# One value load per unit in a buffer of its own, in a cached-attention decode step

## The chip, the cores and the metric

The kernel runs on one core of a Trainium2 chip. The metric is the device time in microseconds of one execution; the time of a kernel is the median of several. A profile is taken from one further execution, and its span (first to last instruction) is a little shorter than that execution's time.

The core has five engines that run side by side and wait for one another by semaphores: TensorE (PE, matmuls; PEld is its weight load), VectorE (DVE), ScalarE (ACT), GpSimd (POOL) and SyncE (SP). Sixteen DMA engines move data between HBM and the on-chip memory, which has 128 partitions.

## The reference

One decode step, one query token for each of two batch entries, mixes cached attention with a gated MLP:

```python
x = A_x                                   # (2, 1, 512)
xn = _layernorm(x, axis=-1)
s = _A_ref(xn, A_k_cache, A_v_cache, A_wq, A_wo)
g = _silu(_B_ref(xn, B_w1, B_w2, B_w3, B_w4))
return x + s * g
```

In `_A_ref`, `q = x @ wq` has 32 heads of 128, and the caches have 8 heads of 32768 tokens by 128, so four query heads share a cache head. Scores are scaled by 128 ** -0.5, a softmax runs over the 32768 tokens, the result is multiplied with V and then with `wo` (4096 x 512). K and V are bfloat16, 2 x 8 x 32768 x 128 each, 134 MB apiece. With one token, the shifted branch of `_B_ref` contributes nothing, so the MLP is what remains: layernorm, `w3` (512 x 1792), gelu, `w4` (1792 x 512), a residual, then silu.

## The kernel before

**Units and pieces.** A unit is one batch entry and one cache head: 16 units, each with 8 MB of K and 8 MB of V. K and V of a unit come in two pieces of 16384 tokens (`NCH` is 2), 4 MB each. In a piece partition p holds 128 tokens that follow one another, 32 KB per partition, so a piece is one contiguous 4 MB of HBM.

**Loads and buffers.** The list `loads` (built ahead of `issue`) gives the order of all large transfers: K of unit 0 with `wq` between its pieces, `w3`, `w4`, and then for each unit n by turns a piece of K of unit n + 1 and a piece of V of unit n, at last `wo`. All are issued on SP's queue and share one pool of five buffers of 32 KB per partition (`SLOTS`). `issue(i)` takes the next buffer in turn, so a load waits until the load five places earlier has been used up. The main loop works through `loads` in the same order and calls `issue(i + SLOTS)` after each. The last V piece goes as two transfers of 2 MB, and `wo` as four (2, 1, 0.5 and 0.5 MB).

**Work on a K piece (`k_job`).** DVE transposes it in four blocks (`transposed`, L286, into `ktb`, two buffers). PE multiplies each block with the query weights `qz`, eight matmuls of 128x512 to a block (`scores`, L234), one block behind DVE (`LAG`). Scores of a unit collect in PSUM. After the last block `softmax_front` takes the row maxima (L248) and appends two steps to a list, `glue`: `step1` transposes the maxima on PE (L253) and reduces them, `step2` broadcasts the maximum (L264), runs the exponentials on ACT (L271) and transposes the probabilities on DVE (L275). `k_job` pops one step of `glue` after each block.

**Work on a V piece (`v_job`).** PE multiplies the piece with the probabilities, 32 matmuls (L313), four column strips of the array at a time. After the first four of them it flushes the K blocks that are still waiting for their scores. After the second piece `unit_end` copies the accumulator (`acs`, L335) and appends the unit's finish (`ot`, L339 to L346) to `glue`.

**Order.** The order of instructions on each engine is the order in which the code issues them (`manual_schedule`). An instruction that waits holds up everything behind it on its engine, and the same goes for a DMA issue on SP.

**Start and end.** The query (`q_job`) is made once the first two K blocks are transposed; the MLP (`mlp_job`, L407 to L439) runs when `w4` is in, between K of unit 0 and K of unit 1. At the end `o_final` reorders the heads, `wo_job` (L365) multiplies with `wo`, and the gated sum goes out.

The functions that the change touches, with what calls them:

Of the kernel before, what the change touches and what calls it, by code (L numbers as in the profile page):

```python
# [9 lines left out]
BF16 = mybir.dt.bfloat16  # L10
# [4 lines left out]

UT = 128
GT = 16
SLOTS = 5
KTB = 2
KG = 2  # L20
LAG = 1
# [3 lines left out]
def kernel(  # L25
# [14 lines left out]
    nc = tc.nc  # L40

    B, Sq, D = A_x.shape
    _, Hkv, Sk, Dh = A_k_cache.shape
    HD = A_wq.shape[1]
    Hq = HD // Dh
    rep = Hq // Hkv
    Fdim = B_w3.shape[1]
    assert Sq == 1 and B == 2 and Dh == 128 and rep == 4 and D == 512 and Fdim % 128 == 0
    DK = D // 128
    FK = Fdim // 128  # L50
    CH = UT * 128
    NCH = Sk // CH
    NB = UT // GT
    NS = 32 // rep
# [8 lines left out]
    NU = len(units)  # L63

    ctx.enter_context(tc.manual_schedule())
    head = ctx.enter_context(tc.tile_pool(name="head", bufs=1))
    slots = ctx.enter_context(tc.tile_pool(name="slots", bufs=SLOTS))
    pers = ctx.enter_context(tc.tile_pool(name="pers", bufs=1))
    kt_pool = ctx.enter_context(tc.tile_pool(name="ktb", bufs=KTB))
    p_pool = ctx.enter_context(tc.tile_pool(name="prob", bufs=2))  # L70
# [10 lines left out]
    w3_v = B_w3.rearrange("(p k) f -> p k f", k=DK)  # L81
    w4_v = B_w4.rearrange("(p f) d -> p f d", f=FK)
    NR = HD // 128
    wo_v = A_wo.rearrange("(p r) d -> p (r d)", r=NR)

    loads = [("K", 0, 0), ("wq",)]
    loads += [("K", 0, c) for c in range(1, NCH)]
    loads += [("w3",), ("w4",)]
    for n in range(NU):
        for c in range(NCH):  # L90
            if n + 1 < NU:
                loads.append(("K", n + 1, c))
            loads.append(("V", n, c))
    wo_cuts = [0, NR // 2, 3 * NR // 4, NR - 4, NR]
    loads += [("wo",)]
    tiles = {}

    def issue(i):
        if i >= len(loads):
            return  # L100
        what = loads[i]
        t = slots.tile([128, UT * Dh], BF16, tag="slot", name=f"slot_{what[0]}")
        if what[0] in ("K", "V"):
            b, g = units[what[1]]
            c = what[2]
            src = A_k_cache if what[0] == "K" else A_v_cache
            sv = src[b, g, c * CH:(c + 1) * CH, :].rearrange("(p t) d -> p (t d)", p=128)
            w = UT * Dh // 2 if what == ("V", NU - 1, NCH - 1) else UT * Dh
            for w0 in range(0, UT * Dh, w):
                nc.sync.dma_start(out=t[:, w0:w0 + w], in_=sv[:, w0:w0 + w])  # L110
        elif what[0] == "wq":
            nc.sync.dma_start(
                out=t[:, 0:DK * HD].rearrange("p (k f) -> p k f", k=DK), in_=wq_v)
        elif what[0] == "wo":
            for r0, r1 in zip(wo_cuts, wo_cuts[1:]):
                nc.sync.dma_start(out=t[:, r0 * D:r1 * D], in_=wo_v[:, r0 * D:r1 * D])
        elif what[0] == "w3":
            nc.sync.dma_start(
                out=t[:, 0:DK * Fdim].rearrange("p (k f) -> p k f", k=DK), in_=w3_v)
        else:  # L120
            nc.sync.dma_start(
                out=t[:, 0:FK * D].rearrange("p (f d) -> p f d", f=FK), in_=w4_v)
        tiles[what] = t

    issue(0)
    x_bf = tmp.tile([B, D], BF16, tag="row", name="x_bf")
    nc.scalar.dma_start(out=x_bf[:, :], in_=A_x[:, 0, :])
    x4 = pers.tile([128, 128], BF16)
    nc.gpsimd.memset(x4[:, :], 0.0)
    for b in range(B):  # L130
        nc.scalar.dma_start(out=x4[b:128:32, :], in_=A_x[b, 0, :].rearrange("(j c) -> j c", j=4))
    for i in range(1, SLOTS):
        issue(i)


    ident = head.tile([128, 128], BF16)
# [10 lines left out]
    for k in range(4):  # L147
        wb, par = k // 2, k % 2
        src = ident[:, :].rearrange("p (wb w two) -> p wb two w", wb=2, two=2)[:, wb, par, :]
# [7 lines left out]
        out=headm[:, :], in_=identf[:, :].rearrange("p (x h) -> p h x", h=rep), axis=AX.X, op=ALU.max)  # L157
# [39 lines left out]
    for j, src in enumerate((xn_bf, ln2_bf)):  # L197
        sv = src[:, :].rearrange("b (p k) -> b k p", k=DK)
        for k in range(DK):
            nc.tensor.transpose(  # L200
                out=treg[:, (j * DK + k) * B:(j * DK + k + 1) * B],
                in_=sv[:, k, :], identity=ident[0:B, 0:B])
# [11 lines left out]
    unit_st = {}  # L214
    waiting = []
    glue = []
# [73 lines left out]
    def flush(keep):  # L290
        while len(waiting) > keep:
            scores(*waiting.pop(0))
# [10 lines left out]
            if glue:  # L303
                glue.pop(0)()

    def v_job(n, c):
        vv = tiles[("V", n, c)][:, :].rearrange("p (e i t d) -> p e t i d", i=4, t=GT, d=Dh)
        for e in range(NB // 4):
            half, r0 = (c * NB + e * 4) // NS, (c * NB + e * 4) % NS * rep
            pT = unit_st[n]["pT"]  # L310
            for t in range(GT):
                j = t % 4
                nc.tensor.matmul(  # L313
                    acc[32 * j:32 * j + 16, :].rearrange("p (i d) -> p i d", d=Dh),
                    lhsT=pT[:, half * GT + t, r0:r0 + 16],
                    rhs=vv[:, e, t, :, :],
                    start=(c == 0 and e == 0 and t < 4),
                    stop=(c == NCH - 1 and e == NB // 4 - 1 and t >= GT - 4),
                    tile_position=(0, 32 * j),
                )  # L320
                if e == 0 and t == 3:
                    flush(0)
                elif t % 4 == 3 and glue and n == NU - 1:
                    glue.pop(0)()
        if c == NCH - 1:
            unit_end(n)

    s_ps = s_psp.tile([128, 128], F32)
# [31 lines left out]
    def wo_job():  # L360
        w = tiles[("wo",)]
        for r in range(NR):
            for j in range(4):
                c0 = r * D + 128 * j
                nc.tensor.matmul(  # L365
                    s_ps[32 * j:32 * j + B, :], lhsT=oP[:, :, r], rhs=w[:, c0:c0 + 128],
                    start=(r == 0), stop=(r == NR - 1), tile_position=(0, 32 * j))
# [31 lines left out]
                out=qz[32 * i:32 * i + 32, n % 2, :, c0:c0 + rep], in_=qp[32 * i:32 * i + 32, :, b, g, :])  # L399

    def mlp_job():
        w3 = tiles[("w3",)][:, 0:DK * Fdim].rearrange("p (k q f) -> p k f q", k=DK, f=FK)
        w4 = tiles[("w4",)][:, 0:FK * D].rearrange("p (f d) -> p f d", f=FK)
        hT_ps = mi_psp.tile([128, FK * B], F32, tag="mi", name="hT")
        for f in range(FK):
            for k in range(DK):
                nc.tensor.matmul(  # L407
                    hT_ps[:, f * B:(f + 1) * B],
                    lhsT=w3[:, k, f, :],
                    rhs=xT[:, DK + k, :],  # L410
                    start=(k == 0), stop=(k == DK - 1),
                )
        hf = pers.tile([128, FK * B], F32)
        nc.vector.tensor_copy(out=hf[:, :], in_=hT_ps[:, :])
        x2 = pers.tile([128, FK * B], F32)
        nc.vector.tensor_mul(out=x2[:, :], in0=hf[:, :], in1=hf[:, :])
        nc.vector.tensor_scalar(out=x2[:, :], in0=x2[:, :], scalar1=0.044715, scalar2=1.0, op0=ALU.mult, op1=ALU.add)
        inner = pers.tile([128, FK * B], F32)
        nc.vector.tensor_mul(out=inner[:, :], in0=hf[:, :], in1=x2[:, :])
        th = pers.tile([128, FK * B], F32)  # L420
        nc.scalar.activation(out=th[:, :], in_=inner[:, :], func=ACT.Tanh, scale=GELU_C)
        nc.vector.tensor_scalar(out=th[:, :], in0=th[:, :], scalar1=0.5, scalar2=0.5, op0=ALU.mult, op1=ALU.add)
        h_bf = pers.tile([128, FK * B], BF16)
        nc.vector.tensor_mul(out=h_bf[:, :], in0=hf[:, :], in1=th[:, :])  # L424
        h2_ps = mi_psp.tile([B, D], F32, tag="mi", name="h2")
        for f in range(FK):
            nc.tensor.matmul(  # L427
                h2_ps[0:B, :],
                lhsT=h_bf[:, f * B:(f + 1) * B],
                rhs=w4[:, f, :],  # L430
                start=(f == 0), stop=(f == FK - 1),
            )
        t_f = tmp.tile([B, D], F32, tag="row", name="t_f")
        nc.vector.tensor_add(out=t_f[:, :], in0=xn[:, :], in1=h2_ps[0:B, :])
        sig = tmp.tile([B, D], F32, tag="row", name="sig")
        nc.scalar.activation(out=sig[:, :], in_=t_f[:, :], func=ACT.Sigmoid)
        nc.vector.tensor_mul(out=g_sb[:, :], in0=t_f[:, :], in1=sig[:, :])
        for b in range(B):
            nc.scalar.dma_start(  # L439
                out=g4[b:128:32, :], in_=g_sb[b:b + 1, :].rearrange("b (j c) -> b j c", j=4))  # L440


    for i, what in enumerate(loads):
        if what[0] == "K":
            k_job(what[1], what[2])
        elif what[0] == "V":
            if what[2] == 0:
                while glue and unit_st[what[1]]["pT"] is None:
                    glue.pop(0)()
            v_job(what[1], what[2])  # L450
        elif what == ("w4",):
            mlp_job()
        elif what[0] == "wo":
            while glue:
                glue.pop(0)()
            o_final()
            wo_job()
        issue(i + SLOTS)

    sg = tmp.tile([128, 128], F32, tag="row", name="sg")  # L460
    nc.vector.tensor_tensor(out=sg[:, :], in0=s_ps[:, :], in1=g4[:, :], op=ALU.mult)
# [34 lines left out]
```

## Time and profile before

| what | value |
|---|---|
| median of three runs | 661.0 us (660.96 to 661.13) |
| the profiled execution | 660.7 us |
| its span | 658.9 us |
| granted TensorE clock, mean | 0.82 |
| data read from HBM | 280.50 MB |
| 4 MB loads of K / V | 32 / 31, and two of 2 MB of V |
| median from issue to landing, K / V | 39.9 us / 34.3 us |

A page of the profile gives each engine's busy time and share of the span, then the span in 40 equal slices with one digit of busy share for each, then DMA queues with packets, megabytes and the share of the 16 engines' time that their packets took. The stage table gives, for each stretch of the span, the busy time of PE, PEld, DVE, ACT and POOL, the granted clock, the DMA share and GB/s. In the timeline a line begins with start and length in us; SPq is SP's queue issuing a DMA; what stands in brackets is how long the engine had been idle and what ended that.

### The profile page before, as it was taken

What the parts mean: (1) busy time and instruction counts of PE and PEld (TensorE: products, weight loads), DVE (VectorE), ACT (ScalarE), POOL (GpSimd) and SP (SyncE); (2) the same over time, 40 slices, a digit from 0 to 9 for tenths busy, and PEclk for the clock granted to TensorE, in tenths of its full rate; (3) what the DMA queues carried; (4) which work ended last, traced back from release to release, by engine and by line L of the source; (5) the groups of instructions that cost most, each with busy time, mean ns of one, the idle gap of its engine ahead of it and who ended that gap; (6) DMA issues with size and microseconds to landing.
All of it is one profiled execution on the core that took longest, in us unless ns stands there. A gap on an engine that the chain in (4) does not pass through costs nothing.

```text
span 658.9 us, 5935 instructions
## 1 busy us (share of the span) xinstructions
PE 420.9 (64%) x2595; PEld 173.8 (26%) x2595; DVE 365.4 (55%) x312; ACT 38.5 (6%) x104; POOL 2.2 (0%) x10
## 2 busy tenths in 40 slices
PE   0587767477575657746567784657668565764775
PEld 0342223132221223222122332223222222322233
DVE  6174856556654645655555654555565455465531
ACT  1103010000000000000000000000000100000000
POOL 1000000000000000000000000000000000000000
PEclk9997877987786898777898686888868688887776
DMA  9999999999999999999999999999999999999995
GB/s 382 420 438 441 417 444 433 426 443 420 442 431 430 439 426 437 432 427 442 427 436 429 430 443 424 437 432 430 443 422 437 432 431 438 425 436 437 430 425 246
DMA packets 10445, 280.88 MB, mean 426 GB/s; under 512 B 1194, under 2 KB 1204, under 8 KB 1460
## 3 DMA queue, kind: packets, MB, share of 16 engines
q1 hardware_dynamic: 10376, 280.50, 98.8%
q8 instruction: 20, 0.33, 0.2%
q14 instruction: 5, 0.04, 0.0%
q10 hardware_dynamic: 44, 0.01, 0.0%
HBM read 280.50 MB, written 0.00 MB: 426 GB/s over the span
## 4 chain that ended last, share of the span: by engine, by line
DMA 71%; PE 17%; DVE 9%; issue 1%; ACT 1%; SPq 0%; DVEq 0%; ACTq 0%
DMA slot_K<-in_A_k_cache_dram 62%; PE sc L234 12%; DVE ktb L286 7%; DMA slot_wo<-in_A_wo_dram 6%; DMA slot_wq<-in_A_wq_dram 3%; PE acc L313 3%; DVE pT L275 1%; ACT pr L271 1%; PE h L427 1%; PE qT L374 1%; PE hT L407 1%; PE bc L264 0%; DVE nb L268 0%; ACT qz L398 0%; DVE Sm L278 0%
## 5 line engine op out<-in xcount | busy, mean ns | idle before, releaser
L234 PE MATMUL sc<-ktb,qz 128*128 128x512 bf16 x1024 | 310.9, 460 | 198.4 <-DVE ktb L286 196.7
L286 DVE STREAM_TRANSPOSE ktb<-slot_K 128x2048 uint32<-128x2048 uint32 x128 | 292.1, 2298 | 169.9 <-DMA slot_K<-in_A_k_cache_dram 142.3
L234 PEld LDWEIGHTS <-qz 128*128 128x128 bf16 x1024 | 110.7, 112 | 369.0 <-issue 305.6
L313 PE MATMUL acc<-slot_V,pT 128*16 128x512 bf16 x1024 | 70.8, 399 | 5.4 <-DMA slot_V<-in_A_v_cache_dram 5.4
L313 PEld LDWEIGHTS <-pT 128*16 128x16 bf16 x1024 | 23.2, 90 | 54.9 <-issue 34.6
L248 DVE TENSOR_REDUCE m<-sc 128x1 f32<-128x1024 f32 x16 | 19.5, 1221 | 29.8 <-PE sc L234 29.8
L398 ACT COPY qz<-qp 32x16 bf16<-32x16 bf16 x64 | 12.9, 201 | 330.0 <-PE sc L234 308.3
L275 DVE STREAM_TRANSPOSE pT<-pr 128x1024 bf16<-128x1024 bf16 x16 | 19.9, 1245 | 21.2 <-ACT pr L271 21.2
L271 ACT ACTIVATE pr<-sc,nb 128x1024 bf16<-128x1024 f32 x16 | 17.8, 1113 | 234.1 <-DVE nb L268 234.1
L335 DVE COPY acs<-acc 128x512 f32<-128x512 f32 x16 | 11.1, 692 | 14.1 <-PE acc L313 14.1
L341 PE MATMUL ot<-sel,acs 128*128 128x4 f32 x128 | 18.2, 265 | 0.3 <-DVE acs L335 0.3
L341 PEld LDWEIGHTS ot<-sel,acs 128*128 128x128 f32 x128 | 17.2, 209 | 0.4 <-DVE acs L335 0.4
L268 DVE TENSOR_SCALAR nb<-bc 128x1 f32<-128x1 f32 x16 | 2.5, 158 | 22.4 <-PE bc L264 22.4
L374 PE MATMUL qT<-xT,slot_wq 128*128 128x2 bf16 x128 | 3.6, 165 | 12.1 <-DMA slot_wq<-in_A_wq_dram 12.1
L264 PEld LDWEIGHTS bc<-ones_f,gx 1*128 1x128 f32 x32 | 6.5, 250 | 12.9 <-issue 10.9
L264 PE MATMUL bc<-ones_f,gx 1*128 1x1 f32 x32 | 7.8, 311 | 1.0 <-DVE gx L258 1.0
L339 PEld LDWEIGHTS ot<-Sm,ones_f 128*128 128x128 f32 x32 | 6.2, 203 | 3.8 <-issue 1.7
L253 PE MATMUL mT<-identf,m 128*1 128x128 f32 x16 | 4.4, 276 | 3.6 <-DVE m L248 3.6
L374 PEld LDWEIGHTS <-slot_wq 128*128 128x128 bf16 x128 | 3.5, 104 | 12.2 <-DMA slot_wq<-in_A_wq_dram 12.2
L427 PE MATMUL h<-slot_w,h_bf 128*2 128x512 bf16 x14 | 4.9, 525 | 1.6 <-DVE h_bf L424 1.6
L345 DVE RECIPROCAL rc<-ot 128x4 f32<-128x4 f32 x16 | 2.4, 149 | 5.5 <-PE ot L341 5.5
L200 PE MATMUL treg<-ident,xn_bf 2*128 2x2 bf16 x4 | 0.3, 174 | 7.8 <-DVE xn_bf L188 7.8
(70 smaller groups left out, 62.4 us busy)
## 6 DMA issues: line engine op xcount, KB each, us to landing
slot_K<-in_A_k_cache_dram SPq DMA_DIRECT2D x32, 4096.0 KB, 39.9
slot_V<-in_A_v_cache_dram SPq DMA_DIRECT2D x31, 4096.0 KB, 34.3
slot_wq<-in_A_wq_dram SPq DMA_DIRECT2D x1, 4096.0 KB, 21.4
slot_V<-in_A_v_cache_dram SPq DMA_DIRECT2D x2, 2048.0 KB, 29.5
slot_w<-in_B_w_dram SPq DMA_DIRECT2D x2, 1792.0 KB, 39.0
slot_wo<-in_A_wo_dram SPq DMA_DIRECT2D x1, 2048.0 KB
slot_wo<-in_A_wo_dram SPq DMA_DIRECT2D x1, 1024.0 KB
slot_wo<-in_A_wo_dram SPq DMA_DIRECT2D x2, 512.0 KB, 38.7
```

What stands on the lines that cost most here:

```text
L234: nc.tensor.matmul(sc[:, half, :].rearrange("p (t k) -> p t k", k=32), lhsT=qz[:, n % 2, k, off:off + 128], rhs=kv[:, k // 2, k % 2, :, :] ...
L248: nc.vector.tensor_reduce(out=m1[:, :], in_=st["sc"][:, :, :].rearrange("p x k -> p (x k)"), axis=AX.X, op=ALU.max)
L264: nc.tensor.matmul(bc[:, :], lhsT=st["gx"][:, :, :].rearrange("o x h -> o (x h)"), rhs=ones_f[0:1, 0:1], start=True, stop=True)
L271: nc.scalar.activation(out=pr[:, :], in_=st["sc"][:, :, :].rearrange("p x k -> p (x k)"), func=ACT.Exp, bias=nb[:, 0:1], scale=inv_sqrt_dh ...
L275: nc.vector.transpose(out=pT[:, :, :].rearrange("p t r -> p (t r)"), in_=pr[:, :])
L286: nc.vector.transpose(out=ktb[:, :], in_=kw)
L313: nc.tensor.matmul(acc[32 * j:32 * j + 16, :].rearrange("p (i d) -> p i d", d=Dh), lhsT=pT[:, half * GT + t, r0:r0 + 16], rhs=vv[:, e, t, ...
L335: nc.vector.tensor_copy(out=acs[:, :], in_=acc[:, :])
L341: nc.tensor.matmul(ot[:, 0:rep], lhsT=acs[:, i * Dh:(i + 1) * Dh], rhs=sel[:, i, :], start=(i == 0), stop=(i == 3))
L374: nc.tensor.matmul(qT_ps[:, h * B:(h + 1) * B], lhsT=w[:, k * HD + h * Dh:k * HD + (h + 1) * Dh], rhs=xT[:, k, :], start=(k == 0), stop=(k ...
L398: nc.scalar.copy(out=qz[32 * i:32 * i + 32, n % 2, :, c0:c0 + rep], in_=qp[32 * i:32 * i + 32, :, b, g, :])
L427: nc.tensor.matmul(h2_ps[0:B, :], lhsT=h_bf[:, f * B:(f + 1) * B], rhs=w4[:, f, :], start=(f == 0), stop=(f == FK - 1),)
```

## The change

V of a unit comes in one load of 8 MB, 64 KB per partition, into a buffer of its own (`vslot`, one buffer of 64 KB per partition). K keeps three buffers of 32 KB (`KSLOTS`). The sum, 160 KB per partition, is that of the five buffers before.

- In a unit partition p now holds 256 tokens that follow one another. A V row is 64 KB of contiguous HBM; a K piece takes 32 KB out of each 64 KB.
- The order of loads becomes: both pieces of K of unit n + 1, then V of unit n.
- `wq`, `w3` and `w4` share the V buffer at different columns ahead of the first V.
- The last unit's V (now called `Z`) comes into K's buffers: one piece of 4 MB, then the second piece as two transfers of 2 MB into one buffer, and `wo` into the third.
- A load is issued when the buffer that it takes has been used up, in the order of the list (`ready`, `issue_ready`). A V load thus waits for the work on the V before it, and the loads behind it in the list wait too.
- Ahead of a unit's V matmuls, the waiting K blocks get their scores and all of `glue` is popped. Then the 64 matmuls follow in one run.

```diff
-SLOTS = 5
+KSLOTS = 3
...
-    slots = ctx.enter_context(tc.tile_pool(name="slots", bufs=SLOTS))
+    slots = ctx.enter_context(tc.tile_pool(name="slots", bufs=KSLOTS))
+    vslot = ctx.enter_context(tc.tile_pool(name="vslot", bufs=1))
...
+    W3, W4 = DK * HD, DK * HD + DK * Fdim
...
     for n in range(NU):
-        for c in range(NCH):
-            if n + 1 < NU:
-                loads.append(("K", n + 1, c))
-            loads.append(("V", n, c))
+        if n + 1 < NU:
+            loads += [("K", n + 1, c) for c in range(NCH)]
+        if n + 1 < NU:
+            loads.append(("V", n))
+        else:
+            loads += [("Z", n, c) for c in range(NCH)]
...
-    def issue(i):
-        if i >= len(loads):
-            return
-        what = loads[i]
-        t = slots.tile([128, UT * Dh], BF16, tag="slot", name=f"slot_{what[0]}")
-        if what[0] in ("K", "V"):
+    kload = [w for w in loads if w[0] in ("K", "Z", "wo")]
+    done = set()
+
+    def ready(what):
+        if what[0] in ("K", "Z", "wo"):
+            j = kload.index(what)
+            return j < KSLOTS or kload[j - KSLOTS] in done
+        if what[0] == "V":
+            return ("V", what[1] - 1) in done if what[1] else ("w4",) in done
+        return True
+
+    def issue_ready():
+        while loads and ready(loads[0]):
+            issue(loads.pop(0))
+
+    def issue(what):
+        if what[0] in ("K", "Z", "wo"):
+            t = slots.tile([128, UT * Dh], BF16, tag="slot", name=f"slot_{what[0]}")
+        elif what[0] in ("wq", "V"):
+            t = vslot.tile([128, NCH * UT * Dh], BF16, tag="v", name=f"slot_{what[0]}")
+        else:
+            t = tiles[("wq",)]
+        if what[0] in ("K", "V", "Z"):
             b, g = units[what[1]]
-            c = what[2]
             src = A_k_cache if what[0] == "K" else A_v_cache
-            sv = src[b, g, c * CH:(c + 1) * CH, :].rearrange("(p t) d -> p (t d)", p=128)
-            w = UT * Dh // 2 if what == ("V", NU - 1, NCH - 1) else UT * Dh
-            for w0 in range(0, UT * Dh, w):
-                nc.sync.dma_start(out=t[:, w0:w0 + w], in_=sv[:, w0:w0 + w])
+            sv = src[b, g, :, :].rearrange("(p t) d -> p (t d)", p=128)
+            if what[0] == "V":
+                nc.sync.dma_start(out=t[:, :], in_=sv)
+            else:
+                c0, w = what[2] * UT * Dh, UT * Dh
+                if what == ("Z", NU - 1, NCH - 1):
+                    w = w // 2
+                for w0 in range(0, UT * Dh, w):
+                    nc.sync.dma_start(out=t[:, w0:w0 + w], in_=sv[:, c0 + w0:c0 + w0 + w])
...
-    def v_job(n, c):
-        vv = tiles[("V", n, c)][:, :].rearrange("p (e i t d) -> p e t i d", i=4, t=GT, d=Dh)
-        for e in range(NB // 4):
-            half, r0 = (c * NB + e * 4) // NS, (c * NB + e * 4) % NS * rep
+    def v_job(n, t, c0, c1):
+        nx = NB // 4
+        vv = t[:, :].rearrange("p (x i t d) -> p x t i d", i=4, t=GT, d=Dh)
+        for x in range(c0 * nx, c1 * nx):
+            half, r0 = x * 4 // NS, x * 4 % NS * rep
...
-                if e == 0 and t == 3:
-                    flush(0)
-                elif t % 4 == 3 and glue and n == NU - 1:
-                    glue.pop(0)()
-        if c == NCH - 1:
+        if c1 == NCH:
             unit_end(n)
...
-    for i, what in enumerate(loads):
+    for what in order:
         if what[0] == "K":
             k_job(what[1], what[2])
         elif what[0] == "V":
-            if what[2] == 0:
-                while glue and unit_st[what[1]]["pT"] is None:
-                    glue.pop(0)()
-            v_job(what[1], what[2])
+            flush(0)
+            while glue:
+                glue.pop(0)()
+            v_job(what[1], tiles[what], 0, NCH)
+        elif what[0] == "Z":
+            while glue:
+                glue.pop(0)()
+            v_job(what[1], tiles[what], what[2], what[2] + 1)
...
-        issue(i + SLOTS)
+        done.add(what)
+        issue_ready()
```

More of the change, by code (lines that the diff above doesn't have):

```diff
@@ L118, in issue @@
             nc.sync.dma_start(
-                out=t[:, 0:DK * Fdim].rearrange("p (k f) -> p k f", k=DK), in_=w3_v)
+                out=t[:, W3:W3 + DK * Fdim].rearrange("p (k f) -> p k f", k=DK), in_=w3_v)
         else:
             nc.sync.dma_start(
-                out=t[:, 0:FK * D].rearrange("p (f d) -> p f d", f=FK), in_=w4_v)
+                out=t[:, W4:W4 + FK * D].rearrange("p (f d) -> p f d", f=FK), in_=w4_v)
         tiles[what] = t
-    issue(0)
+    order = list(loads)
+    issue(loads.pop(0))
     x_bf = tmp.tile([B, D], BF16, tag="row", name="x_bf")
@@ L131 @@
         nc.scalar.dma_start(out=x4[b:128:32, :], in_=A_x[b, 0, :].rearrange("(j c) -> j c", j=4))
-    for i in range(1, SLOTS):
-        issue(i)
+    issue_ready()
     ident = head.tile([128, 128], BF16)
@@ L304, in k_job @@
                 glue.pop(0)()
-    def v_job(n, c):
-        vv = tiles[("V", n, c)][:, :].rearrange("p (e i t d) -> p e t i d", i=4, t=GT, d=Dh)
-        for e in range(NB // 4):
-            half, r0 = (c * NB + e * 4) // NS, (c * NB + e * 4) % NS * rep
+    def v_job(n, t, c0, c1):
[3 more added lines that the diff above has]
+            half, r0 = x * 4 // NS, x * 4 % NS * rep
             pT = unit_st[n]["pT"]
-            for t in range(GT):
-                j = t % 4
+            for u in range(GT):
+                j = u % 4
                 nc.tensor.matmul(
                     acc[32 * j:32 * j + 16, :].rearrange("p (i d) -> p i d", d=Dh),
[L315 to L318, printed above, removed]
+                    lhsT=pT[:, half * GT + u, r0:r0 + 16],
+                    rhs=vv[:, x - c0 * nx, u, :, :],
+                    start=(x == 0 and u < 4), stop=(x == NCH * nx - 1 and u >= GT - 4),
                     tile_position=(0, 32 * j),
                 )
-                if e == 0 and t == 3:
-                    flush(0)
-                elif t % 4 == 3 and glue and n == NU - 1:
-                    glue.pop(0)()
-        if c == NCH - 1:
+        if c1 == NCH:
             unit_end(n)
@@ L401, in mlp_job @@
     def mlp_job():
-        w3 = tiles[("w3",)][:, 0:DK * Fdim].rearrange("p (k q f) -> p k f q", k=DK, f=FK)
-        w4 = tiles[("w4",)][:, 0:FK * D].rearrange("p (f d) -> p f d", f=FK)
+        w3 = tiles[("w3",)][:, W3:W3 + DK * Fdim].rearrange("p (k q f) -> p k f q", k=DK, f=FK)
+        w4 = tiles[("w4",)][:, W4:W4 + FK * D].rearrange("p (f d) -> p f d", f=FK)
         hT_ps = mi_psp.tile([128, FK * B], F32, tag="mi", name="hT")
@@ L457 @@
             wo_job()
-        issue(i + SLOTS)
+        done.add(what)
+        issue_ready()
     sg = tmp.tile([128, 128], F32, tag="row", name="sg")
```

## The prediction

> **What bounds the kernel now.** I read the page's three summary rows first, then the stage table, then the end of the chain, then the order of time at the two places where the new buffers could bite.
>
> The page (busy totals, the 40 slices, the queues):
>
> ```profile
> span 658.9 us, 5935 instructions
> PE 420.9 (64%) x2595; PEld 173.8 (26%) x2595; DVE 365.4 (55%) x312; ACT 38.5 (6%) x104; POOL 2.2 (0%) x10
> ...
> DMA  9999999999999999999999999999999999999995
> ...
> q1 hardware_dynamic: 10376, 280.50, 98.8%
> ...
> HBM read 280.50 MB, written 0.00 MB: 426 GB/s over the span
> ```
>
> No compute engine is busy two thirds of the time; the SP queue's packets fill 98.8% of the 16 DMA engines' span. The stage table (us; PE, PEld, DVE, ACT and POOL busy; granted clock; DMA share; GB/s) shows that this is no average over good and bad stretches:
>
> ```profile
> 60.00:640.00 580.00, 379.52 (x2142) 151.32 (x2146) 331.69 (x260) 30.56 (x85) 0.00 (x0) 0.81 1.00 432
> 0.00:60.00 60.00, 30.06 (x274) 15.65 (x274) 31.62 (x46) 7.98 (x20) 2.21 (x10) 0.97 0.98 419
> 640.00:650.00 10.00, 7.43 (x58) 3.69 (x51) 0.87 (x2) 0.00 (x0) 0.00 (x0) 0.50 0.98 417
> ```
>
> The DMA share is 1.00 for 580 us on end. So the time is the bytes at the engines' own pace, plus about 2 us ahead of the first packet and 4 us behind the last. The chain's last pieces (start, length, what) say what the end waits for:
>
> ```profile
> 616.18 38.74 DMA slot_wo<-in_A_wo_dram
> 654.92 0.04 issue
> 654.97 0.42 PE s_ps L365 x16
> ```
>
> The last quarter-load of wo lands, 16 matmuls run, the output goes out. For the pace itself I used the packet records that the trace holds behind the DMA rows. On the engine that is first to finish, a 4 MB load follows the one before by 9.681 us all the way, a 2 MB load by 4.862 us; a 32 KB packet took 1213 ns in the median and at the 5th and 95th percentile, a 4-byte completion packet 9 ns. The engine that is last runs 0.4 us behind at first and 4.4 us behind at the end, in steps that fall beside the 20 instruction fetches of 16 KB.
>
> **The change, part by part.** Bytes, matmuls, transposes and softmax steps are the same in number. What can move the time is the DMA work and whether the engines always have work queued.
>
> *One V load for two (15 units).* Two halves of 16 KB rows cost 2 x 4.862 = 9.724 us where one load of 32 KB rows costs 9.681: a load carries 0.043 us that don't scale with bytes (8 packets and a completion per engine). By the same step, joining two 4 MB loads into one with 64 KB rows saves 0.043 us, 15 x 0.043 = 0.65 us in all, on the bound itself. No row has a 64 KB packet. If each row is still moved as two packets, only the completion goes: 15 x 9 ns = 0.14 us. If the whole fixed part of a packet's recorded time goes (159 ns for 4 KB and 1213 for 32 KB put it at 8 ns), the gain is 15 x (8 x 8 + 9) ns = 1.1 us. I take 0.65, the measured spacing, and keep 0.1 and 1.1.
>
> A rule bears on this place. The Trainium skill, "DMA: Bandwidth & Descriptors", section "Anatomy of one DMA", gives each DMA about 2 us besides its bytes. By that rule 15 loads fewer would be an estimated 30 us and the time 631. The trace disagrees: loads follow one another at 9.681 us, so that part lies under the loads queued ahead.
>
> *Rows 64 KB apart.* K pieces now take 32 KB of each 64 KB, V rows lie 64 KB apart. The nearest rows are the strided loads of before: the V halves and the first wo piece, 16 KB out of each 32 KB, cost 4.863 and 4.862 us, no more than half a contiguous load plus the 0.043. I take no cost. No row shows a 64 KB pitch. As the bad end I take the spread of the rate itself: between 60 and 640 us the slowest slice before the last had 428 GB/s against 433 typical, 1.2%; on K's and V's 268 MB (620 us at 433 GB/s) that is +7 us. No gain is on offer here: packets of one size already take one time, whatever the load.
>
> The skill has a rule against this part. The same page, section "Latency and other measured facts", has copies at a 512 KiB row pitch at 207 GB/s against 214 with padding. By its 3% this kernel would lose an estimated 20 us; nothing in this trace shows a loss with pitch.
>
> *One V buffer.* This adds a wait: V of unit n+1 is issued only when the last of V n's 64 matmuls is done. SP queues both K loads of the unit after behind it, so PE and DVE would starve in turn. Is it ever late? Let V n's last byte land at t. Behind it are queued two K loads, 19.4 us, up to t + 19.4, on the engine that is first up to t + 15.0 (19.4 less the 4.4 above). V's matmuls: 28 took 1.69 us at full clock (60 ns each), 40 took 4.44 us at half clock (111 ns); 64 take 3.9 to 7.1 us. They can begin at t + 0.4 (the lag from last packet to first use), if PE is there. K n+1's two pieces landed at t - 29.0 and t - 19.4. How long a piece takes is shown here (start, length, engine, what):
>
> ```profile
> 304.88 4.50 DVE L286 STREAM_TRANSPOSE ktb<-slot_K 128x2048 uint32<-128x2048 uint32 x2 [6.92 <-DMA slot_K<-in_A_k_cache_dram]
> ...
> 310.51 4.50 DVE L286 STREAM_TRANSPOSE ktb<-slot_K 128x2048 uint32<-128x2048 uint32 x2 [1.13 <-PE sc L234]
> ...
> 317.00 1.22 DVE L248 TENSOR_REDUCE m<-sc 128x1 f32<-128x1024 f32 x1 [1.99 <-PE sc L234]
> ```
>
> One piece is 12.1 us at mixed clock, V work of 0.4 us included. Two are done at t - 4.8, the softmax front that now all runs ahead of V (reduce 1.2, two transposes and copies, about 3 us) at t - 1.8, the finish of the unit before, 1.2 us of PE, at t - 0.6. So the next V is issued by t + 7.5; from issue to first packet was 1.0 us (0.73 to 1.75 for the first load). 8.5 against 15.0: 6.5 us to spare in the middle, at half clock. DVE's next transposes stand behind V's accumulator copy, which ends by t + 8.3; their K lands at t + 9.7. Hidden.
>
> The start is tighter, since the MLP holds up K of unit 1:
>
> ```profile
> 50.43 4.87 PE L427 MATMUL h<-slot_w,h_bf 128*2 128x512 bf16 x14 [1.63 <-DVE h_bf L424]
> ...
> 55.33 0.33 SPq L110 DMA_DIRECT2D slot_K<-in_A_k_cache_dram  x1
> ...
> 72.34 2.31 DVE L286 STREAM_TRANSPOSE ktb<-slot_K 128x2048 uint32<-128x2048 uint32 x1 [0.35 <-PE sc L234]
> ```
>
> V 0 reuses wq's buffer, so it goes out when the MLP's last matmul is done: 55.33, where before a K load went. First packet 56.4; K 1's second piece, now queued ahead, ends at 59.4 on the first engine. 3.0 us to spare. V 1 needs V 0's matmuls: K 1's second piece starts on DVE at 72.34 as before, before, its last score ended at 85.5, with 2.7 us of V 0's matmuls among its own that are now behind; so 82.8 to 85.5, then the softmax front, 3 us, and V, 3.9 to 7.1: issue at 89.7 to 95.6. The queue would run dry on the first engine at 98.1 (59.4 plus four times 9.681); the late end leaves 98.1 - 1.0 - 95.6 = 1.5 us. Cost nothing; a late one costs what it is late by, once.
>
> *K's three slots.* K n+2's second piece needs K n+1's first transposed: about t - 17, wanted by t + 9.7. The first K of unit 1 waits for nothing but K 0's landing, and K 1's second piece for K 0's transposes (36.97, as a load did before). Hidden.
>
> *SP and PE order.* SP issues 15 DMAs fewer at 0.33 us; it stood waiting 374.6 us for DVE alone. PE loses the interleaving of V with K; it idles anyway.
>
> *The end.* The last unit's V keeps the pieces of before (4, 2, 2 MB), and wo follows in its four. V 14 lands at 625.4, takes until 633, its finish 2 us; the first piece of V 15 lands at 635. After the last half the steps are those of before. PE finished the first 112 wo matmuls at 654.32, 0.65 us ahead of the last landing; both shift together.
>
> **Sum.** The profiled execution took 660.7 us, its span 658.9 and 1.8 around it. Span 658.9 - 0.65 = 658.25, execution 660.05. The median of the three runs is 661.0, 0.3 above the profiled one; on it, 660.35, so 660.4.
>
> **Rivals.**
> - *Rows cut into two packets*: gain 0.14, 660.9. For it: no 64 KB packet is seen in the trace. Against: every contiguous row up to 32 KB went as one packet (8192 of 32 KB).
> - *A luckier last engine*: its 4.4 us lag is made mostly of about 0.95 us steps. One fewer on that engine gives 660.4 - 0.95 = 659.4. For it: packets twice as long shift which fetch meets which. Against: the instruction count stays, and so should the fetches.
> - *V starves the queue* (slower): the single V buffer is freed too late, after t + 14 in the middle. For it: PE at half clock for a whole unit, and the 1.5 us margin at V 1. Against: the 6.5 us above. One missed microsecond in each of 14 units gives 674.4; at V 1 alone, 661.4.
> - *Pitch* (slower): +7 us, 667.6 from the 660.4. Against: the strided rows above.
>
> **How the numbers follow.** No change can be told within 0.2%, 659.7 to 662.3. Main case 0.60; two packets 0.12, both within. Luckier engine 0.13: faster. Starving 0.09 and pitch 0.06: slower. So faster 0.13, same 0.72, slower 0.15. The range 659.3 to 663.0 holds the main case with its 0.1 and 1.1 ends (660.9 and 659.9), the luckier engine and a single late V of up to 2 us; beyond it lie repeated starving and pitch.
>
> **What would show it.** Right: V packets of 64 KB at about 2417 ns, q1 at 8216 packets (10376 less 15 x 128 and 15 x 16 completions; 10136 where rows are cut), DMA share still 1.00 between 60 and 640 us, wo landing about 0.65 us sooner, and SP's V loads issued within 9 us of landing. Wrong: slices under 425 GB/s in the middle, PE or DVE waiting for K right after a V load that was issued late, or 32 KB packets over 1213 ns.

## The result, and the profile after

| | before | after |
|---|---|---|
| median, 22 runs each | 661.02 us (660.60 to 661.29) | 660.06 us (659.90 to 660.44) |
| ratio | | 0.9987, 95% interval 0.9981 to 0.9993 |
| the profiled execution, its span | 660.7, 658.9 us | 659.9, 658.1 us |
| granted TensorE clock, mean | 0.82 | 0.82 |

A second measurement of the changed kernel, beside the last experiment, gave 660.19 us against 660.94: 0.9989 (0.9980 to 0.9998). So it is faster by 0.75 and 0.96 us in the two, about a tenth of a per cent, within the 0.2% that the prediction called no change. The forecast was 660.4.

The page of the changed kernel, in the same parts as before (the first lines, two queues, and the chain by line):

```profile
span 658.1 us, 5904 instructions
PE 413.4 (63%) x2595; PEld 176.8 (27%) x2595; DVE 364.0 (55%) x312; ACT 38.5 (6%) x104; POOL 2.2 (0%) x10
...
DMA  9999999999999999999999999999999999999995
GB/s 383 423 436 446 417 465 423 412 457 408 460 412 428 461 404 453 417 445 426 423 458 411 450 424 437 432 423 444 427 443 418 456 405 444 443 416 457 406 427 248
...
q1 hardware_dynamic: 8216, 280.50, 98.8%
q8 instruction: 20, 0.33, 0.2%
...
DMA slot_V<-in_A_v_cache_dram 59%; PE acc L338 11%; DMA slot_K<-in_A_k_cache_dram 7%; DMA slot_wo<-in_A_wo_dram 6%; DVE ktb L310 2%; PE sc L258 1%; DVE m L272 0%; SPq L140 0%; PE bc L288 0%; PE s_ps L385 0%; DVE acs L355 0%; DVE sg L486 0%; DVE out_bf L488 0%; DVE gm L279 0%; PE mT L277 0%
```

8216 packets: exactly the number for V rows that go as single packets of 64 KB. The packet records show 1920 of them (15 x 128), 2418 ns in the median and at the 5th and 95th percentile.

The chain now names PE's V matmuls (acc, L338) for 11% of the span. That is no loss. The chain walks back from a V load to what released its issue, and that is now the V matmuls before it; it doesn't ask whether the DMA engines had other work meanwhile. The stage table does (columns as in the prediction; DMA share and GB/s are the last two):

```profile
60.00:640.00 580.00, 373.35 (x2154) 154.96 (x2158) 331.02 (x261) 31.18 (x86) 0.00 (x0) 0.82 1.00 432
0.00:60.00 60.00, 30.54 (x274) 15.68 (x274) 30.89 (x45) 7.37 (x19) 2.21 (x10) 0.94 1.00 427
640.00:650.00 10.00, 6.02 (x43) 3.16 (x35) 1.28 (x4) 0.00 (x0) 0.00 (x0) 0.50 0.98 415
```

The share is 1.00 over the same 580 us. And the chain's end:

```profile
616.68 37.51 DMA slot_wo<-in_A_wo_dram
654.24 0.42 PE s_ps L385 x16
```

The 16 matmuls that wait for the last piece of wo start at 654.24, 0.73 us sooner than before (654.97). In the packet records the first engine ends a V load 19.319 us after the K load ahead of it; two V pieces took 2 x 9.681 = 19.362. The difference, 0.043 us, 15 times, is 0.65. In this execution the first load also came in 0.16 us sooner than in the profiled execution of before (first completion 12.02 against 12.18), and one load in the middle came 0.06 us later than its spacing. The early first load is not part of the gain: the run with V in two loads (below) has it too, at 12.07, and starts its last 16 matmuls at 654.97, like the kernel before.

### The profile page after: what moved, and what is told of

The parts are those of the page before. It is cut to its first block, busy times and chain, and to the rows that moved or that the text cites. A ratio compares the mean times of both kernels' runs of the same rounds, so it can differ in the third digit from the quotient of the medians.

```text
span 658.1 us, 5904 instructions
## 1 busy us (share of the span) xinstructions
PE 413.4 (63%) x2595; PEld 176.8 (27%) x2595; DVE 364.0 (55%) x312; ACT 38.5 (6%) x104; POOL 2.2 (0%) x10
## 3 DMA queue, kind: packets, MB, share of 16 engines
q1 hardware_dynamic: 8216, 280.50, 98.8%
## 4 chain that ended last, share of the span: by engine, by line
DMA 72%; PE 13%; issue 3%; DVE 2%; SPq 0%; DVEq 0%
DMA slot_V<-in_A_v_cache_dram 59%; PE acc L338 11%; DMA slot_K<-in_A_k_cache_dram 7%; DMA slot_wo<-in_A_wo_dram 6%; DVE ktb L310 2%; PE sc L258 1%; DVE m L272 0%; SPq L140 0%; PE bc L288 0%; PE s_ps L385 0%; DVE acs L355 0%; DVE sg L486 0%; DVE out_bf L488 0%; DVE gm L279 0%; PE mT L277 0%
## 5 line engine op out<-in xcount | busy, mean ns | idle before, releaser
L258 PE MATMUL sc<-ktb,qz 128*128 128x512 bf16 x1024 | 271.1, 414 | 96.3 <-DVE rc L365 61.3
L310 DVE STREAM_TRANSPOSE ktb<-slot_K 128x2048 uint32<-128x2048 uint32 x128 | 286.7, 2285 | 67.8 <-DMA slot_K<-in_A_k_cache_dram 44.3
L258 PEld LDWEIGHTS <-qz 128*128 128x128 bf16 x1024 | 103.8, 103 | 256.5 <-issue 165.7
L338 PE MATMUL acc<-slot_V,pT 128*16 128x512 bf16 x960 | 85.2, 533 | 71.7 <-DMA slot_V<-in_A_v_cache_dram 71.7
L338 PEld LDWEIGHTS <-pT 128*16 128x16 bf16 x1024 | 33.2, 116 | 130.3 <-issue 122.4
L288 PE MATMUL bc<-ones_f,gx 1*128 1x1 f32 x32 | 6.3, 263 | 9.3 <-DVE gx L282 9.3
L338 PE MATMUL acc<-slot_Z,pT 128*16 128x512 bf16 x64 | 6.4, 556 | 7.4 <-DMA slot_Z<-in_A_v_cache_dram 7.4
L288 PEld LDWEIGHTS bc<-ones_f,gx 1*128 1x128 f32 x32 | 4.9, 192 | 13.0 <-DVE gx L282 12.1
L279 DVE TENSOR_REDUCE gm<-mT 1x4 f32<-1x128 f32 x16 | 4.5, 278 | 5.8 <-PE mT L277 5.8
L447 PE MATMUL h<-slot_wq,h_bf 128*2 128x512 bf16 x14 | 6.0, 622 | 1.6 <-DVE h_bf L444 1.6
```

The source lines that it names most:

```text
L258: nc.tensor.matmul(sc[:, half, :].rearrange("p (t k) -> p t k", k=32), lhsT=qz[:, n % 2, k, off:off + 128], rhs=kv[:, k // 2, k % 2, :, :] ...
L288: nc.tensor.matmul(bc[:, :], lhsT=st["gx"][:, :, :].rearrange("o x h -> o (x h)"), rhs=ones_f[0:1, 0:1], start=True, stop=True)
L310: nc.vector.transpose(out=ktb[:, :], in_=kw)
L338: nc.tensor.matmul(acc[32 * j:32 * j + 16, :].rearrange("p (i d) -> p i d", d=Dh), lhsT=pT[:, half * GT + u, r0:r0 + 16], rhs=vv[:, x - c0 ...
L447: nc.tensor.matmul(h2_ps[0:B, :], lhsT=h_bf[:, f * B:(f + 1) * B], rhs=w4[:, f, :], start=(f == 0), stop=(f == FK - 1),)
```

## Experiments

Theory A: the time is the DMA engines' work, and the gain is the fixed cost of the packets that are gone. Theory B: the order, the buffers or the start made it. The second question is how much cover the single V buffer has, since nothing but cover keeps its new wait at no cost.

### V in two loads again

```diff
-                nc.sync.dma_start(out=t[:, :], in_=sv)
+                for w0 in range(0, 2 * UT * Dh, UT * Dh):
+                    nc.sync.dma_start(out=t[:, w0:w0 + UT * Dh], in_=sv[:, w0:w0 + UT * Dh])
```

> The changed kernel with V of a unit in two loads of 4 MB again, each 32 KB of every 64 KB row, one behind the other into the same buffer; buffers, order and waits stay. Theory A (the fixed cost of packets and loads, 0.043 us a load, made the gain): the gain of 15 x 0.043 goes, 660.7 us, 0.9990 to 1.0000 of the kernel before, and the last wo load lands 0.65 us later than with one load. Theory B (order, buffers or the start made it): the gain stays, 660.1 us. In the packet records, A expects no 64 KB packet and V loads that follow at 9.681 us each on the first engine.

660.88 us, 0.9998 of the kernel before (0.9989 to 1.0006). From its page (span, the SP queue, the issues of V):

```profile
span 659.1 us, 5918 instructions
...
q1 hardware_dynamic: 10376, 280.50, 98.8%
...
slot_V<-in_A_v_cache_dram SPq DMA_DIRECT2D x30, 4096.0 KB, 25.9
```

The packets are back at the 10376 of before, the loads follow at 9.681 us, and the last 16 matmuls start at 654.97, as before. Buffers, order, waits and pitch were the changed kernel's. So without the single load no gain can be told: theory A. B's 660.1 us would be a ratio of 0.9986, outside the interval, and the fastest of this run's 11 executions (660.59 us) is slower than the slowest of the changed kernel's 22 (660.44).

### The 64 KB pitch alone, in the kernel before

```diff
-            sv = src[b, g, c * CH:(c + 1) * CH, :].rearrange("(p t) d -> p (t d)", p=128)
+            sv = src[b, g, :, :].rearrange("(p t) d -> p (t d)", p=128)[:, c * UT * Dh:(c + 1) * UT * Dh]
```

> The kernel before with one part of the change alone: a partition holds 256 tokens that follow one another, so each piece of K and V takes 32 KB out of every 64 KB of HBM; loads, buffers and order are those of before. If a 64 KB pitch costs nothing: 661.0 us, ratio 1.000 within 0.001, 32 KB packets at 1213 ns. If it cost the 1.2% of the prediction's bad end: 668 us.

660.88 us, 0.9998 (0.9989 to 1.0007); 32 KB packets took 1213 ns as before.

```profile
span 658.8 us, 5935 instructions
...
q1 hardware_dynamic: 10376, 280.50, 98.9%
```

A 64 KB pitch costs nothing that can be told here, within about 0.1%. The bad end of the prediction (+7 us) is out. The 3% that the prediction took from the Trainium skill ("DMA: Bandwidth & Descriptors", section "Latency and other measured facts") stands there for copies between HBM tensors at a pitch of 512 KiB; these loads at 64 KB show no such loss, and larger pitches were not tried.

### V in eight loads

```diff
-                nc.sync.dma_start(out=t[:, :], in_=sv)
+                for w0 in range(0, 2 * UT * Dh, UT * Dh // 4):
+                    nc.sync.dma_start(out=t[:, w0:w0 + UT * Dh // 4], in_=sv[:, w0:w0 + UT * Dh // 4])
```

> The changed kernel with V of a unit in eight loads of 1 MB, 8 KB of every 64 KB row each. Theory A: seven loads more in each of 15 units at 0.043 us, +4.6 us on the changed kernel, 664.6 us. Theory B: no change, 660.1 us, as long as the queue is never empty. If each load had a fixed part of 2 us that nothing hides, 105 loads would cost some 210 us.

665.01 us, 1.0059 (1.0047 to 1.0072): 4.95 us over the changed kernel, 0.047 us for each of 105 loads. On the first engine eight of them took 8 x 2.453 = 19.624 us, 0.305 more than the single one, 4.6 in all. So 0.043 us a load holds down to 1 MB loads, as far as the queue is kept full. The Trainium skill, "DMA: Bandwidth & Descriptors", section "Anatomy of one DMA", has about 2 us besides the bytes for one DMA, and by its heading for DMAs that GpSimd issues. For loads that SP issues and that queue behind one another this run shows a fortieth of that.

### One load, 16 packets to a row

```diff
+VPAD = 16
...
+        t = vslot.tile([128, NCH * UT * Dh + 16 * VPAD], BF16, ...)
...
-                nc.sync.dma_start(out=t[:, :], in_=sv)
+                nc.sync.dma_start(
+                    out=t[:, :].rearrange("p (a f) -> p a f", a=16)[:, :, 0:GT * Dh],
+                    in_=sv.rearrange("p (a f) -> p a f", a=16))
```

`VPAD` counts elements of 2 bytes. The view of V in `v_job` steps over the gaps.

> The changed kernel with V of a unit still in one load, but its 64 KB row cut into 16 runs of 4 KB by gaps of 32 bytes in the destination: the number of loads, issues and completions stays, that of packets is 16 times. If of the 0.043 us of a load its 8 packets an engine make nearly all (4.3 ns each), 15 units x 8 rows x 15 more packets x 4.3 ns = +7.7 us on the changed kernel, 667.8 us. If the completion or the load itself makes it, nothing, 660.1 us.

674.76 us, 1.0207 (1.0193 to 1.0221): 14.7 us over the changed kernel with the same 15 loads. Packets cost, then, and not the load alone. But it is 8.2 ns for each of 15 x 8 x 15 extra packets, twice what was expected. One difference was not meant: with gaps of 32 bytes, the packets of a row start 4128 bytes apart, at every multiple of 32 bytes. The next run spaced them by 4224 bytes (`VPAD = 64`).

> As the run with 16 packets to a row, with gaps of 128 bytes in place of 32, so that every packet starts on a multiple of 128 bytes. That run cost 14.7 us over the changed kernel, 8 ns for each extra packet where 4.3 was expected. If the odd starts (multiples of 32 bytes) made the rest: 4.3 ns a packet again, 667.8 us. If the price is that of a packet in a row cut by gaps: 674.8 us again.

669.40 us, 1.0127 (1.0113 to 1.0141): 9.3 us over the changed kernel, 5.2 ns a packet. The page's rows for the two runs, first gaps of 32 bytes, then of 128:

```profile
span 673.0 us, 5904 instructions
...
q1 hardware_dynamic: 37016, 280.50, 99.8%
...
HBM read 280.50 MB, written 0.00 MB: 417 GB/s over the span
```

```profile
span 667.5 us, 5904 instructions
...
q1 hardware_dynamic: 37016, 280.50, 99.7%
...
HBM read 280.50 MB, written 0.00 MB: 420 GB/s over the span
```

Packets, bytes and loads are equal; the spacing of the packets in the buffer makes 5.4 us. In the records the 4 KB packets took 160 ns in the median and 171 at the 95th percentile with gaps of 32 bytes, 159 and 161 with 128. With gaps of 128 bytes, a V load took 19.88 to 19.92 us on the first engine, 0.57 to 0.60 more than with whole rows: 4.7 to 5.0 ns for each of 120 packets. If a packet of an uncut row has the same price, eight of them, 38 to 40 ns, are nearly all of a load's 43.

### V done twice, three times, four times

```diff
-            v_job(what[1], tiles[what], 0, NCH)
+            for _ in range(1):
+                v_job(what[1], tiles[what], 0, NCH, end=False)
+            v_job(what[1], tiles[what], 0, NCH)
```

`range(2)` and `range(3)` for three and four passes; the last pass alone counts, and only it ends the unit. The further passes put off the moment at which the V buffer is free. The changed kernel's own timeline shows that moment at the start (V 0's matmuls, then the issue of V 1) and in the middle, and below stands SP's wait for the V matmuls (us in total, times, longest):

```profile
86.55 5.22 PE L338 MATMUL acc<-slot_V,pT 128*16 128x512 bf16 x64
...
91.81 0.33 SPq L128 DMA_DIRECT2D slot_V<-in_A_v_cache_dram  x1
...
352.95 5.13 PE L338 MATMUL acc<-slot_V,pT 128*16 128x512 bf16 x64 [4.45 <-DMA slot_V<-in_A_v_cache_dram]
...
358.13 0.33 SPq L128 DMA_DIRECT2D slot_V<-in_A_v_cache_dram  x1
...
362.59 2.31 DVE L310 STREAM_TRANSPOSE ktb<-slot_K 128x2048 uint32<-128x2048 uint32 x1 [3.77 <-DMA slot_K<-in_A_k_cache_dram]
```

```profile
SPq L128 <- PE acc L338: 85.9, 14, 11.0
```

In the middle PE has been idle for 4.45 us when its V is there; 64 matmuls later SP issues the next V, and K is still on its way when DVE is free again. In the packet records the first engine had the two K loads behind V done at 97.94 and 368.71, so 5.1 and 9.6 us were left after taking off 1.0 for the start of a load; from V 2 on it was 7.2 to 10.9.

> The changed kernel with the 64 V matmuls of each of the first 15 units done twice (the first pass is overwritten by the second), so a V buffer comes free one pass later, 3.9 to 7.1 us, 5.2 in the middle. In the profile of the changed kernel the next V load was issued 7.2 to 10.9 us before it would have been too late in the middle and 5.1 at V 1. Theory A (the single buffer has cover): no stall in the middle, at V 1 none to 2 us; 660.0 to 662.5 us with the longer program's instruction fetches. Theory B (the single buffer is at its limit, any delay goes straight to the end): 14 x 5.2 = +73 us, 733 us.

> The same with three passes: V comes free 7.8 to 14.2 us later, 10.4 in the middle. Theory A: that is about the cover of 7.2 to 10.9 us, so the queue begins to run dry, 0 to 3 us in each of 14 units, 660 to 705 us. Theory B: +146 us, 806 us.

> The same with four passes: 15.6 us later in the middle. Theory A: 5 to 8 us beyond the cover in each of 14 units, +70 to +112 us, 730 to 772 us, with the DMA share under 1 and SP's V loads issued after the K loads ahead have ended. Theory B: +218 us.

| passes | median us | ratio (95%) | next V issued, us after V landed (from V 2 on) | DMA share, GB/s, 60 to 640 us |
|---|---|---|---|---|
| 1 (the changed kernel) | 660.06 | 0.9987 (0.9981 to 0.9993) | 5.6 to 6.9 | 1.00, 432 |
| 2 | 661.63 | 1.0010 (1.0001 to 1.0019) | 8.9 to 10.4 | 1.00, 432 |
| 3 | 663.82 | 1.0041 (1.0026 to 1.0057) | 12.2 to 13.8 | 1.00, 430 |
| 4 | 677.15 | 1.0247 (1.0232 to 1.0261) | 14.4 to 19.2 | 0.98, 420 |

Theory B's 733, 806 and 878 us are far off: the wait is under cover. The cover ends about where the prediction put it, at 14 us after landing. At three passes the first engine ran dry three times in the middle by 0.8 to 1.3 us, where the issue came 12.7 to 13.8 us after landing; the last engine, which is behind, did not: it followed within 0.01 us of its usual 19.32 there. How the 3.8 us of this run divide between such gaps and its longer program (35 instruction fetches for 20) was not told apart. At four passes it begins with V 1, issued 4.6 us too late, and the last engine loses 5 us there too. The stage table of that kernel, and SP's waits:

```profile
60.00:640.00 580.00, 481.77 (x4732) 213.19 (x4733) 326.37 (x256) 30.13 (x86) 0.00 (x0) 0.94 0.98 420
90.00:110.00 20.00, 17.47 (x246) 8.06 (x238) 8.39 (x7) 0.00 (x0) 0.00 (x0) 1.00 0.79 324
```

```profile
SPq L128 <- PE acc L338: 224.2, 14, 20.6
SPq L128 <- DMA slot_V<-in_A_v_cache_dram: 176.1, 14, 15.6
```

Between 90 and 110 us the DMA share falls to 0.79 while SP waits for the V matmuls, 20.6 us at the longest: this is what the starving rival would have looked like. The wait alone does not tell: the changed kernel's SP waits there too, 14 times, at a DMA share of 1.00. Four passes cost 17 us and not the 70 to 112 expected: a further pass takes about 3.4 us, not 5.2 (see the last section), so V is free some 10 us later, not 15.6.

### More instructions, no later V

Two passes took 1.6 us more with no gap in the middle. Their program is longer by a third, and instructions come through the same DMA engines (q8). In the changed kernel's packet records each of the first 19 of the 20 fetches stands in a hole of 0.86 to 0.97 us, about its own length, in the packets of one engine (engines told apart by packets that follow one another without a gap). The run with two passes has 28 fetches:

```profile
span 659.9 us, 7824 instructions
...
q8 instruction: 28, 0.46, 0.2%
```

The test gives PE as many further instructions where they hold up no buffer:

```diff
             v_job(what[1], tiles[what], 0, NCH)
+            pad = mi_psp.tile([128, 4 * Dh], F32, tag="mi", name="pad")
+            for u in range(64):
+                j = u % 4
+                nc.tensor.matmul(
+                    pad[32 * j:32 * j + 16, :], lhsT=perm[:, 0:4, :].rearrange("p h a -> p (h a)"),
+                    rhs=pick[:, :, :, :].rearrange("p k i w -> p (k i w)"),
+                    start=(u < 4), stop=(u >= 60), tile_position=(0, 32 * j))
```

> The changed kernel with 64 further matmuls behind V's in each of the first 15 units, on constants into a spare PSUM tile that nothing reads: as many PE instructions as the run with V done twice, but V's buffer comes free as before. That run took 1.6 us more than the changed kernel with no stall of the DMA queue in its middle. If its longer program made that (28 instruction fetches of 16 KB for 20, through the same DMA engines): 661.2 to 661.9 us here too. If V's later release made it: 660.1 us.

661.61 us, 1.0012 (1.0003 to 1.0020), with V issued when the changed kernel issues it (6.35 us after landing at the second V load, 6.29 there).

```profile
span 660.0 us, 7824 instructions
...
q8 instruction: 28, 0.46, 0.2%
```

So the 1.6 us (1.4 beside the second measurement of the changed kernel, 660.19) go with the added matmuls and their instructions, and V's later release cost nothing that can be told at two passes. A program longer by a third cost more than the change under study gained. By the last V load only about 0.6 us of it had come about (the first engine 0.37 later, the last 0.26 further behind it); the other 1 us arose in the last 10 us. Both longer programs have a fetch at 649.5 to 649.6, while wo comes in, where the changed kernel has none between 632.8 and 652.3. Whether this fetch makes the 1 us stays open: the records do not name the engine of a packet, and among the short loads of the end the engines can't be told apart surely.

### The changed kernel again

> The changed kernel itself, beside the others on this chip: 660.06 us as measured before, ratio 0.998 to 0.9993; by the sum of the prediction 0.9990.

660.19 us against 660.94, 0.9989 (0.9980 to 0.9998).

## Why the prediction was right

- **The bound** was the 16 DMA engines with a queue that is never empty. It held: a share of 1.00 in the middle before and after, and what an experiment added to the V loads on the first engine came out at the end, or a little more: 4.6 and 4.95 us with eight loads, 8.8 and 9.3 with 16 packets to a row and gaps of 128 bytes.
- **One V load for two**, 0.65 us: 15 x 0.043, and 0.043 is what the first engine's records show for each. The whole gain was 0.75 and 0.96 us, with intervals that hold 0.65; undoing this part alone took it back to within 0.14 us of the kernel before, inside the interval. What lies above 0.65 was not told apart from the spread between executions. The ends (0.1 for cut rows, 1.1) were not needed.
- **The skill's 2 us for each DMA**, weighed against 9.681 us from load to load: the row decided, rightly. By its heading the section cited speaks of DMAs that GpSimd issues, and SP issues these, which the prediction did not say.
- **The pitch** at no cost: shown by its own run. The bad end of 7 us was read from the spread of slices, while the loads of that same execution followed one another at 9.681 us all the way; what the spread of slices is worth, the next point shows.
- **A sign that misled.** "Slices under 425 GB/s in the middle" was to show the prediction wrong, and the GB/s row above has many, down to 404. Yet the DMA share is 1.00, V and K follow at 19.319 and 9.681 us, and in stretches of 40 us from 80 to 640 the rate is 430 to 435 GB/s. A packet counts whole in the slice in which it starts, and a round of 16 packets of 64 KB is 1 MB of the 7 MB in a slice, so a round more or less moves a slice by some 60 GB/s (an estimate from these numbers).
- **The wait of the single V buffer** at no cost: right, with terms that were off both ways. V's 64 matmuls took 5.1 to 6.4 us (3.9 to 7.1 given); PE had been idle for 4.45 us or more when V 1 and those after it were there, where 0.6 us before the landing was given; SP issues the next V 5.6 to 6.9 us after landing (7.5 given), with 7.2 to 10.9 to spare (6.5). V 1 went out at 91.81 (89.7 to 95.6), with 5.1 us to spare (1.5); that is 11.5 us after V 0 landed, so the sign "within 9 us of landing" held from V 2 on only. V 0 went out at 55.95, not 55.33, since the MLP's last matmuls took 6.01 us where they had taken 4.87; K's last piece ended at 59.26, so 2.3 us were left of the 3.0 given.
- **The rivals.** Rows cut in two: no. A luckier last engine: no; it was 4.5 us behind the first at the end, 4.4 before. But what the rival stood on, instruction fetches that hold up one engine, is real, as their holes in the packet records show. Starving: no, and its threshold was well placed.

## What to carry to other kernels

Where the DMA engines have a share of 1.00 over a stretch, price a change there by the spacing of loads that follow one another: here 0.043 us for each load of 128 rows, most of it some 5 ns for each of an engine's 8 packets (8 ns where packets lay 4128 bytes apart), so larger rows were worth a tenth of a per cent and fewer loads next to nothing beyond that. A buffer may be single if what frees it comes before the loads queued behind it have run out; work out that cover from the timeline, at the start as well as in the middle, for what goes beyond it shows: at four passes V 1 was issued 4.6 us too late, and its load ended 5 us later. And count the instructions: each fetch of 16 KB held up one of the same engines for 0.86 to 0.97 us.

## What was not expected

- **The spacing of packets in the buffer.** 4 KB packets 4128 bytes apart cost 5.4 us more over 126 MB than 4224 bytes apart, 2.8 ns for each of an engine's 1920 packets. Other spacings were not tried, nor which property of the spacing makes it.
- **Each V run of the changed kernel begins at half clock, and further passes go mostly at full clock.** In the row from the middle PE had been idle for 4.45 us when V was there; the 64 matmuls took 5.13 us, the first 3 us of it at half clock (four matmuls in 0.43 us), the rest at full (four in 0.22). Over the 15 runs the half clock lasted 3 to 5.5 us of 5.1 to 6.4. In the run with four passes, V 0's 256 matmuls took 15.41 us, 3.4 for each further pass, and the mean granted clock rose with the passes: 0.82, 0.87, 0.91, 0.94. The expectations had taken 5.2 us for each pass, as if each began anew. The Trainium skill, "TensorE: Matmul & The Clock Gate", section "What's actually happening", has the rule that was left out of them: after an idle window of about 3.4 us the clock is halved, and it comes back after about as long of steady work. The runs from V 1 on, after 4.45 to 5.9 us idle, agree with it in the main. In the clock's records the half clock around them lasts 6.83 or 10.24 us, two or three times 3.41. V 0's run, at 86.55, doesn't agree as it stands: half clock was granted from 86.39 for 3.41 us, though PE had not been idle for more than 1.3 us at a stretch since 83.99, with two short groups of matmuls between.
